# A transformer layer whose first two x tiles are loaded transposed and centred through TensorE, with the other second flips of segment 0 by DMA, merged small operations and a new timetable

## The chip, the cores and the metric

One core of a Trainium2 chip runs the whole program. The metric is the device time of one execution in microseconds (us); lower is better. Five engines take part, each with its own queue that runs in order: TensorE (PE, with its weight loads PEld), VectorE (DVE), ScalarE (ACT), GpSimd (POOL) and SyncE (SP). SP issues nearly all DMA transfers, in its own order, and an engine that waits holds up everything behind it on the same queue.

## The reference

The layer is a pre-norm transformer block on 2048 tokens of width 576 with 32 heads of 18. Attention runs over four segments of 512 tokens. In a segment it mixes a causal softmax attention with a read of a compressive memory M that the earlier segments have filled.

```python
h = x + _A_ref(_layernorm(x, axis=-1), A_wq, A_wk, A_wv, A_wo, A_beta)
h2 = h + _B_ref(_layernorm(h, axis=-1), B_w1, B_b1, B_w2, B_b2)
...
for s in range(N):
    p = _softmax(logits, axis=-1)
    a_dot = jnp.einsum('bhqk,bhkd->bhqd', p, vs)
    pq = phi(qs)
    num = jnp.einsum('bhld,bhde->bhle', pq, M)
    den = jnp.einsum('bhld,bhd->bhl', pq, z)[..., None] + 1e-06
    o = g * (num / den) + (1.0 - g) * a_dot
    pk = phi(ks)
    M = M + jnp.einsum('bhld,bhle->bhde', pk, vs)
    z = z + jnp.einsum('bhld->bhd', pk)
```

`phi(t)` is `where(t > 0, t + 1, exp(t))`. `_B_ref` is a feed-forward net 576 to 4608 to 576 with a tanh GELU between.

## The kernel before

A segment s has four token tiles of 128 rows. The work on it goes through named stages, and every operation is recorded with a tag (stage, segment, and for segment 0 a part) and a name:

- X: load x, layer norm (`stats`, `rstd`, `apply`), and the normalized tile `xn` turned into columns. For segment 0 and half of segment 1 the turn is nine TensorE transposes per tile (`TX`) with copies out of PSUM; for the others the tile goes to DRAM and comes back by a transposing DMA (`flip`).
- P: the projections `Pk`, `Pq`, `Pv` (18 matmuls each for a tile, on two halves of the array's rows), copied out of PSUM by ACT or DVE. Segment 0 turns its first q/k tile by TensorE (`TQ`) and the other three by flips; the others go through DRAM (`qkst`). `ek`, `rk`, `fk` make phi(k) for the memory.
- A: scores (`st0`, `st`), softmax exponentials on ACT (`exp`, 80 in all, each 128x2048), causal masks (`mask`, on POOL or DVE), value matmuls (`val`), then a 32x32-block transpose out of PSUM (`valT`), a reciprocal and the gate (`rec`, `rec2`), and sums (`comb`, `comb2`). For segments 1 to 3 the memory read: `eg`, `rg`, `pq` make phi(q), `mem` is its matmul.
- M: the memory update. B: output projection (`Po`, `Ro`), residual, second layer norm, and the turn of its result `xn2` into `x2T`. The result is written twice side by side, once by `apply` and its repetition by a copy named `tail`, since the two row halves of the array read the blocks in two orders. C: first feed-forward matmul `F1`, evictions `copy` with the bias on ACT or DVE, and `gelu` over batches of many blocks. D: second matmul `F2`, then the output.

The order of the work is neither found at run time nor left to a compiler. `TIMETABLE` gives for every operation a rank and an engine letter (p, a, d, g, s for PE, ACT, DVE, POOL, SP); `Graph.schedule` sorts by rank and emits the operations in that order. So each engine's queue has the ranks' order, and the time is decided by what waits for what. `PORT`, `OVER`, `SLIP` and the costs in `add` are the numbers of a planner that made the table; at build time they choose buffers, not the order.

The begin of the program is what the change touches most. x tile 0 arrives in two pieces (SP and ACT queues), tile 1 in one. The mean of a row is summed by ACT and DVE together (`sum`, lines 739 and 741), `apply` subtracts it (line 763), nine transposes (line 777) turn the tile, ACT copies it into `xreg`, and the projections (line 873) begin. The scale 1/sigma of these two tiles is applied later, when ACT or DVE copies the projections out of PSUM (lines 656, 660). A copy of one element called `gate` (line 725) holds the second batch of loads (x tiles 2 and 3, the q weights `hT`) until the first x has landed. Eight or nine large matmuls on zeros (`warm`, lines 671 and 673) run before.

Of the kernel before, what the change touches and what calls it, by code (L numbers as in the profile page):

```python
# [21 lines left out]
LETTERS = dict(p="pe", a="act", d="dve", g="pool", s="sp")  # L22
# [27 lines left out]
    "A03st0": "p 299 252 318 271 335 377 362",  # L50
    "A03swap": "g 401 402",
    "A03val": "p 340 346 382 385",
    "A03valT": "d 347 390",
    "A1comb": "d460 d498 g576 g613 g648 g666 g751 g720",
    "A1comb2": "g489 g535 g579 g636 d659 g697 g754 d726",
    "A1eg": "a 342 429 351 445 599 538 650 686",
    "A1exp": "a 355 417 433 476 456 484 504 443 547 518 608 591 527 638 623 560 682 675 691 653",
    "A1flip": "s 341 426 349 410 501 502 529 632",
    "A1mask": "g411 g440 g418 d451 g449 g491 g490 d470 g526 g531 g539 g540 d500 g567 d559 g554 d624 g605 g592 d566 g604 g651 d652 g640 d620 d684 "
        "g708 g688 g676 g692 d671 g654",  # L60
    "A1mem": "p 409 492 427 533 630 641 714 696",
    "A1memT": "d 412 496 430 537 631 645 715 698",
    "A1memfin": "g479 g532 g448 g634 d655 g689 g753 g718",
    "A1oT": "d 730 735 746 770 764",
    "A1pq": "d 358 431 365 486 606 627 678 687",
    "A1rec": "d 414 499 447 614 639 646 719 702",
    "A1rec2": "d 459 497 544 612 644 665 745 710",
    "A1rg": "g 357 428 364 485 542 626 555 679",
    "A1st": "p 344 413 432 466 455 483 503 441 546 511 607 590 525 637 622 558 681 667 690 649",
    "A1swap": "g 727 747",  # L70
    "A1val": "p 452 494 541 580 633 662 728 704",
    "A1valT": "d 458 495 543 581 643 663 733 706",
    "A2comb": "d837 d900 d942 g929 d963 g1027 d1061 g1085",
    "A2comb2": "g838 g904 d960 d930 d967 d1029 g1075 g1090",
    "A2eg": "a 768 716 755 828 912 898 945 1014",
    "A2exp": "a 729 737 760 705 771 881 848 834 878 871 903 928 917 972 954 978 956 1010 1018 1040",
    "A2flip": "s 707 617 709 742 823 830 920 882",
    "A2mask": "g738 d752 d756 g761 g763 g721 g788 g772 g893 g868 d894 d854 g889 d879 d888 g872 g943 g952 d939 d918 d982 d980 g965 d979 g985 g973 "
        "g1002 g1035 g1053 g1056 g1079 g1041",
    "A2mem": "p 791 741 905 842 931 1008 1015 1086",  # L80
    "A2memT": "d 792 744 907 843 935 1011 1024 1087",
    "A2memfin": "d795 g821 d958 d906 g966 g1028 g1074 d1089",
    "A2oT": "d 994 995 1030 1096 1104",
    "A2pq": "d 775 717 874 833 913 990 1007 1072",
    "A2rec": "d 793 762 908 844 936 1020 1026 1088",
    "A2rec2": "d 827 861 941 922 962 998 1060 1082",
    "A2rg": "g 748 642 713 783 909 953 959 1063",
    "A2st": "p 725 736 759 703 769 880 845 829 873 850 886 927 914 971 948 977 955 1006 1017 1039",
    "A2swap": "g 1098 1091",
    "A2val": "p 824 825 896 890 957 983 1037 1080",  # L90
    "A2valT": "d 826 840 940 915 961 993 1038 1081",
    "A3comb": "d1155 g1205 g1275 d1245 d1349 g1362 d1441 d1417",
    "A3comb2": "d1183 g1206 d1305 d1254 d1352 g1400 d1450 g1429",
    "A3eg": "a 1036 1109 1214 1167 1185 1319 1267 1383",
    "A3exp": "a 1103 1118 1067 1100 1084 1221 1231 1176 1200 1187 1303 1250 1276 1291 1256 1331 1342 1350 1369 1334",
    "A3flip": "s 981 1057 1102 934 1134 1152 1261 1309",
    "A3mask": "g1133 g1145 g1142 g1114 g1159 g1128 g1158 g1143 g1229 g1248 g1243 g1246 g1210 g1223 d1194 d1236 g1311 d1280 g1268 g1277 g1297 g1323 "
        "g1310 d1308 g1421 d1394 d1395 g1413 d1360 g1406 d1351 g1396",
    "A3mem": "p 1165 1139 1251 1203 1312 1327 1412 1409",
    "A3memT": "d 1168 1140 1257 1204 1313 1328 1414 1420",  # L100
    "A3memfin": "g1182 d1148 g1273 d1237 d1336 d1399 d1419 d1424",
    "A3oT": "d 1306 1307 1401 1452 1455",
    "A3pq": "d 1116 1131 1215 1174 1258 1320 1343 1408",
    "A3rec": "d 1177 1147 1260 1235 1316 1332 1418 1423",
    "A3rec2": "d 1153 1198 1263 1244 1321 1361 1440 1416",
    "A3rg": "g 1108 1105 1141 1169 1195 1262 1339 1366",
    "A3st": "p 1101 1117 1059 1097 1083 1218 1230 1175 1199 1186 1298 1238 1272 1290 1255 1315 1341 1347 1368 1333",
    "A3swap": "a1433 g1453",
    "A3val": "p 1146 1160 1249 1239 1317 1324 1422 1407",
    "A3valT": "d 1149 1197 1259 1240 1318 1355 1432 1415",  # L110
    "B00Po": "p 219",
    "B00Ro": "p 223",
    "B00T": "p 274 284",
    "B00apply": "d 267",
    "B00copy": "d 275 285",
    "B00dma": "s 210",
    "B00hadd": "d 224 227",
    "B00pass": "d 220",
    "B00rstd": "g 266",
    "B00stats": "d 253",  # L120
    "B00tail": "g 273",
    "B01Po": "p 225",
    "B01Ro": "p 232",
    "B01T": "p 276 286",
    "B01apply": "d 256",
    "B01copy": "d 277 287",
    "B01dma": "s 233",
    "B01hadd": "d 237 238",
    "B01pass": "d 226",
    "B01rstd": "g 255",  # L130
    "B01stats": "d 239",
    "B01tail": "d 257",
    "B02Po": "p 463",
# [12 lines left out]
    "B03dma": "s 468",
    "B03flip": "s 589",
    "B03hadd": "d 514 516",
    "B03pass": "g 507",
    "B03rstd": "g 548",  # L150
    "B03stats": "d 521",
    "B03tail": "g 588",
    "B1Po": "p 778 779 856 777",
    "B1Ro": "p 782 789 864 790",
    "B1apply": "d 851 892 933 816",
    "B1dma": "s 757 812 836 794",
    "B1flip": "s 860 921 938 887",
    "B1hadd": "d 784 785 813 814 869 870 796 797",
    "B1pass": "g781 d780 g863 g787",
    "B1rstd": "g 835 891 897 811",  # L160
    "B1stats": "d 786 815 895 798",
    "B1tail": "g859 d911 g937 d853",
    "B2Po": "p 1123 1120 1274 1122",
    "B2Ro": "p 1129 1137 1283 1126",
    "B2apply": "d 1213 1266 1292 1224",
    "B2dma": "s 1154 1062 1253 1031",
    "B2flip": "s 1220 1357 1356 1281",
    "B2hadd": "d 1156 1157 1138 1144 1284 1285 1150 1151",
    "B2pass": "d1127 d1121 g1282 d1125",
# [12 lines left out]
    "B3tail": "g1515 d1561 g1564 g1536",
# [1376 lines left out]
```

## Time and profile before

| what | value |
|---|---|
| median of 3 runs | 449.36 us (448.22 to 450.42) |
| the profiled execution | 449.18 us, of which the profile's span is 447.5 us |
| PE busy | 431.5 us, 96% of the span |
| ACT, DVE, POOL busy | 301.2, 286.9, 180.8 us |
| TensorE clock granted | 1.00 |
| DMA moved | 63.41 MB, mean 142 GB/s |

A profile row reads "start us, duration us, engine, line, operation, out<-in, count [idle before <- what ended it]". Lines of the kernel stand as L873 and so on. PE's rows are pipelined: a row's duration includes the drain, so the distance from one row's start to the next is the better price of a group of matmuls.

### The profile page before, as it was taken

The numbers are of one execution on the slowest core, as the hardware profiler recorded it, in microseconds if no ns is written. First come the engines' busy times: TensorE is split into PE (matmuls) and PEld (weight loads), VectorE is DVE, ScalarE is ACT, GpSimd is POOL, SyncE is SP. The second block draws the span as 40 slices with busy tenths as digits, with TensorE's granted clock in tenths as the row PEclk, the third lists the DMA queues.
The fourth block names the chain that finished last, engine by engine and source line by source line (L and its number), as shares of the span: only waits on it lengthen the run. The fifth ranks groups of instructions, "written<-read, shape, count | busy, mean of one in ns | idle before, by whom it ended". The sixth has DMA issues, their size and how long they took to land. (4 is left out here: it accounts for less than half of the span.)

```text
span 447.5 us, 12499 instructions
## 1 busy us (share of the span) xinstructions
PE 431.5 (96%) x5345; PEld 278.9 (62%) x5346; DVE 286.9 (64%) x623; ACT 301.2 (67%) x261; POOL 180.8 (40%) x319
## 2 busy tenths in 40 slices
PE   6987999899999999999999999999999999999997
PEld 4766677656776676664444766654447775445775
DVE  6899888999889877795678688773774322000012
ACT  6887999898978798775898977563787002566000
POOL 5683867668355833651235265520212111000001
PEclk9999999999999999999999999999999999999999
DMA  7669869999899944861657505404503281340001
GB/s 226 173 134 219 302 216 210 244 260 247 174 285 221 318 159 95 147 130 25 186 162 153 140 4 103 91 4 130 173 1 94 68 198 44 128 149 1 0 15 41
DMA packets 78344, 63.41 MB, mean 142 GB/s; under 512 B 62288, under 2 KB 70096, under 8 KB 78288
## 3 DMA queue, kind: packets, MB, share of 16 engines
q1 hardware_dynamic: 78144, 62.52, 54.9%
q8 instruction: 42, 0.69, 0.7%
q10 hardware_dynamic: 144, 0.09, 0.1%
q14 instruction: 14, 0.11, 0.1%
HBM read 37.36 MB, written 10.29 MB: 106 GB/s over the span
## 5 line engine op out<-in xcount | busy, mean ns | idle before, releaser
L1185 ACT ACTIVATE pt<-bank 128x2048 bf16<-128x2048 f32 x60 | 112.5, 1876 | 32.8 <-PE bank L1181 26.9
L1398 PEld LDWEIGHTS <-hT 128*128 128x128 bf16 x1152 | 110.5, 98 | 34.7 <-issue 6.6
L1312 PE MATMUL bank<-xreg,w1g 64*128 64x512 bf16 x972 | 107.2, 376 | 0.0
L1312 PEld LDWEIGHTS <-w1g 64*128 64x128 bf16 x972 | 46.3, 94 | 57.3 <-issue 2.8
L1398 PE MATMUL bank<-w_lo,hT 128*128 128x288 bf16 x576 | 77.8, 286 | 0.2 <-issue 0.2
L1398 PE MATMUL bank<-w,hT 128*128 128x288 bf16 x576 | 76.8, 286 | 0.6 <-DVE ot L1409 0.6
L1409 DVE TENSOR_TENSOR ot<-bank,hc 128x288 bf16<-128x288 f32 x32 | 14.3, 452 | 90.5 <-PE bank L1398 86.6
L873 PE MATMUL bank<-hT,xreg 64*128 64x288 bf16 x864 | 58.9, 283 | 4.8 <-DMA hT<-in_A_w_dram 2.1
L1196 POOL TENSOR_SCALAR_AFFINE_SELECT pt<-pt 128x512 bf16<-128x512 bf16 x67 | 45.1, 688 | 30.6 <-ACT pt L1185 30.3
L873 PEld LDWEIGHTS <-xreg 64*128 64x128 bf16 x864 | 42.8, 94 | 17.1 <-issue 8.5
L1317 ACT ACTIVATE hT<-bank,b_col 128x512 bf16<-128x512 f32 x36 | 22.6, 687 | 45.6 <-PE bank L1312 45.3
L1327 DVE TENSOR_SCALAR hT<-bank,b_col 128x512 bf16<-128x512 f32 x42 | 30.1, 742 | 21.4 <-PE bank L1312 20.2
L1384 POOL TENSOR_TENSOR hc<-h,b_bc 128x288 f32<-128x288 bf16 x16 | 12.4, 774 | 76.9 <-DVE ot L1409 76.9
L1027 ACT ACTIVATE pt<-bank 128x2048 bf16<-128x2048 f32 x20 | 37.5, 1877 | 6.2 <-PE bank L1024 5.5
L1349 PE MATMUL bank<-xreg,w1g 64*128 64x256 bf16 x648 | 38.6, 269 | 0.5 <-DVE qk_pad L662 0.3
L1349 PEld LDWEIGHTS <-w1g 64*128 64x128 bf16 x648 | 30.8, 94 | 7.0 <-issue 3.6
L1332 ACT ACTIVATE hT<-hT 128x8192 bf16<-128x8192 bf16 (+2 forms) x6 | 31.7, 5318 | 0.2 <-DVE hT L1327 0.2
L1325 ACT ACTIVATE hT<-bank,b_col 128x512 bf16<-128x512 f32 x30 | 19.5, 685 | 16.2 <-PE bank L1312 15.9
L1181 PE MATMUL bank<-qk 32*128 32x384 bf16 (+3 forms) x384 | 23.8, 300 | 1.6 <-DVE v_aug L662 0.9
L753 POOL TENSOR_SCALAR ln<-ln 128x1 f32<-128x1 f32 x32 | 8.8, 277 | 39.2 <-DVE ln L750 39.0
L1226 POOL TENSOR_TENSOR o_nat<-t,t 128x288 bf16<-128x288 f32 x13 | 10.6, 816 | 28.0 <-DVE t L1167 20.4
L1145 DVE SCALAR_TENSOR_TENSOR e<-e,r 128x512 bf16<-128x512 bf16 x24 | 18.9, 788 | 4.0 <-ACT e L1141 3.5
(119 smaller groups left out, 564.2 us busy)
## 6 DMA issues: line engine op xcount, KB each, us to landing
w1g<-in_B_w_dram SPq DMA_DIRECT2D x41, 576.0 KB, 4.4
qkd<-qk_pad SPq DMA_DIRECT2D x12, 512.0 KB, 4.8
w_lo<-in_B_w_dram SPq DMA_DIRECT2D x3, 864.0 KB, 6.6
w<-in_B_w_dram SPq DMA_DIRECT2D x3, 864.0 KB, 6.6
xb<-in_A_x_dram SPq DMA_DIRECT2D x16, 144.0 KB, 3.8
out_dram<-ot SPq DMA_DIRECT2D x15, 144.0 KB, 1.8
x<-in_A_x_dram SPq DMA_DIRECT2D x6, 320.0 KB, 4.5
xnd<-xn SPq DMA_DIRECT2D x10, 160.0 KB, 3.1
```

The costliest lines, as they stand in the source:

```text
L873: nc.tensor.matmul(out=c.t[:, w, 0:HALF], lhsT=xTb.t[r, k, ts], rhs=wt[r, k, :], start=(k == 0), stop=(k == ND - 1))
L1027: ex = add(ps, {"act": 1.88}, lambda e: nc.scalar.activation(out=pt.t[:], in_=st.t[:], func=ACT.Exp, scale=scale), [sc], pt, [st], table=" ...
L1181: nc.tensor.matmul(out=st.t[:, i, off:off + n_], lhsT=qk[rows, 1, kt * P:(kt + 1) * P], rhs=qk[rows, 0, kt * P:L], start=True, stop=True, ...
L1185: ex = add(ps, {"act": 1.88}, lambda e, st=st, pt=pt: nc.scalar.activation(out=pt.t[:], in_=st.t[:], func=ACT.Exp, scale=scale), [sc], pt, ...
L1196: nc.gpsimd.affine_select(out=blk, in_=blk, pattern=[[0, 4], [1, P]], compare_op=ALU.is_ge, fill=0.0, base=0, channel_multiplier=-1)
L1312: nc.tensor.matmul(out=cc[w].t[:], lhsT=w1.t[rows, k, q, :], rhs=x2T[s].t[rows, k, :], start=(k == 0), stop=(k == ND - 1))
L1317: ready_f[f + w] = [add(pf - 12, {"act": 0.68}, lambda e, f=f, w=w, cc=cc: nc.scalar.activation(out=hT[:, :, f + w, :], in_=cc[w].t[:].rea ...
L1325: nc.scalar.activation(out=dst, in_=src, func=ACT.Identity, bias=b)
L1327: nc.vector.tensor_scalar(out=dst, in0=src, scalar1=b, scalar2=None, op0=ALU.add)
L1332: ge = add(2.9, {"act": 0.42 * (f1 - f0) + 0.2}, lambda e, f0=f0, f1=f1: nc.scalar.activation(out=hT[:, :, f0:f1, :], in_=hT[:, :, f0:f1, ...
L1349: nc.tensor.matmul(out=cc[w].t[:, q * 2 * P:(q + 1) * 2 * P], lhsT=w1.t[rows, k, q, :], rhs=x2T[s].t[rows, k, ts], start=(k == 0), stop=(k ...
L1398: nc.tensor.matmul(out=c.t[:, 0:HALF], lhsT=hT[:, tl // 2, f, (tl % 2) * P:(tl % 2 + 1) * P], rhs=w2_c[ch][:, f - ch * WCH, hf * HALF:(hf ...
```

## The change

It has five parts.

1. Segment 0's tiles 0 and 1 come from a second, transposed copy of x, `A_xt`, which the host lays out, straight into `xreg`. TensorE multiplies them by ones (five matmuls for a tile, `cs`), which leaves the column sums on every partition, and DVE subtracts the mean in place (`ctr`, two instructions for a tile). `sum`, `mean`, `apply`, 18 transposes and their copies go. The untransposed rows of both tiles are still loaded (`x01`), for the variance. The warm-up writes ones in place of zeros, one call of it goes, and DVE does the gate's copy.
2. The second norm's result of segment 0, tiles 0 and 1, is turned by flips, as tiles 2 and 3 were; 18 transposes and 4 copies go. `apply` writes both copies of `xn2` in one instruction, on DVE or POOL, and `tail` goes.
3. Small operations are merged or split: the gate factor of `rec2` moves into `comb` (one instruction on DVE, two on POOL); the wide masks of segment 0 become halves.
4. More operations may run on POOL or DVE as the table says: `phi` for `fk` and `pq` on POOL (two instructions there), `apply` of x on POOL, `rk` and `rg` on DVE.
5. The letter t: 24 evictions of C1 and C2 apply the GELU directly on ACT, and the batches leave these blocks out. The whole timetable is new (1704 ranks before, 1688 now), with new planner numbers.

```diff
-    "X00TX": "p 21 22 26 35",
-    "B00T": "p 274 284",
+    "X00cs": "p 11 13",
+    "B00flip": "s 242",
...
-        warm_ok = add(-9.5, {"dve": 0.25}, lambda e: nc.vector.memset(warm[:], 0.0), name="memset")
+        warm_ok = add(-9.5, {"dve": 0.25}, lambda e: nc.vector.memset(warm[:], 1.0), name="memset")
...
-        fill = [warm_up(2, 1.08, [wprev], [Buf(c_s)], 2 * P), warm_up(2, 0.86, [wprev], [Buf(c_s)])]
+        fill = [warm_up(2, 0.86, [wprev], [Buf(c_s)])]
...
+        xt0 = load(-7.9, lambda: xtv(0, 0, KT), lambda: xt_src(0, 0, KT), 164e3, acq=xt)
+        x0b = add(-7.85, {"act": 1.69}, lambda e: nc.scalar.dma_start(out=xtv(0, KT, ND), in_=xt_src(0, KT, ND)), (), None, [xt], name="x0b")
...
+        x1 = add(-7.5, {"sp": 0.45}, lambda e: nc.sync.dma_start(out=xtv(1, 0, ND), in_=xt_src(1, 0, ND)), (), None, [xt], size=295e3, name="x1")
...
+        x01 = add(-7.45, {"sp": 0.45}, lambda e: nc.sync.dma_start(out=x0.t[:], in_=x[0:2 * P, :].rearrange("(j p) d -> p j d", p=P)), (), x0, size=325e3, name="x01")
...
+                    def sums(e, c=c, tl=tl):
+                        for k in range(KT):
+                            r = slice(0, 64 if k == KT - 1 else P)
+                            nc.tensor.matmul(out=c.t[:, 0:P], lhsT=warm[r, 0:P], rhs=xtv(tl, k, k + 1)[r, 0, :], start=(k == 0), stop=(k == KT - 1))
+
+                    def centre(e, k0, k1, c=c, tl=tl):
+                        nc.vector.scalar_tensor_tensor(out=xtv(tl, k0, k1), in0=c.t[:, 0:P].unsqueeze(1).to_broadcast([P, k1 - k0, P]), scalar=-1.0 / D,
+                                                       in1=xtv(tl, k0, k1), op0=ALU.mult, op1=ALU.add)
...
+        def phi(e, out, ek, rk):
+            if e == "dve":
+                nc.vector.scalar_tensor_tensor(out=out, in0=ek, scalar=1.0, in1=rk, op0=ALU.min, op1=ALU.add)
+                return
+            nc.gpsimd.tensor_scalar(out=ek, in0=ek, scalar1=BIG, scalar2=1.0, op0=ALU.min, op1=ALU.min)
+            nc.gpsimd.tensor_tensor(out=out, in0=ek, in1=rk, op=ALU.add)
...
-                    nc.vector.tensor_scalar(out=r1.t[:], in0=r1.t[:], scalar1=omg_q[:, g:g + 1], scalar2=None, op0=ALU.mult)
...
+                        nc.vector.scalar_tensor_tensor(out=t1.t[:, :, 0:Dh], in0=t1.t[:, :, 0:Dh], scalar=omg_q[:, g:g + 1], in1=rb, op0=ALU.mult, op1=ALU.mult)
...
-                ap = layernorm(p0, lambda h=h: h.t[:], [prev], h, xn2, 0.48, later)
-                by_dma = s > 0 or tl in DMA_FLIP_0
...
+                ap = layernorm(p0, lambda h=h: h.t[:], [prev], h, xn2, 0.60, later, twice=True)
...
-                                    nc.scalar.activation(out=dst, in_=src, func=ACT.Identity, bias=b)
+                                    nc.scalar.activation(out=dst, in_=src, func=ACT.Gelu_apprx_tanh if me[0].straight else ACT.Identity, bias=b)
```

DVE, the first rows of the program. `ln` holds the norm's sums, `x_64` is the buffer of tiles 0 and 1 in rows, `xn` the centred tile, `xreg` the transposed tiles, `pt_71` the warm-up's operand. Before:

```order
L636 MEMSET mhalf 128x1
L666 MEMSET pt_71 128x256
L636 MEMSET v_aug_112 128x128
L741 TENSOR_REDUCE ln_102<-x_64 128x1
L744 TENSOR_SCALAR ln_102<-ln_102 128x1
L763 TENSOR_SCALAR xn_139<-x_64,ln_102 128x640
L741 TENSOR_REDUCE ln_103<-x_64 128x1
L744 TENSOR_SCALAR ln_103<-ln_103 128x1
L763 TENSOR_SCALAR xn_140<-x_64,ln_103 128x640
L749 BN_STATS ln_103<-x_64 128x6 x2
```

The same place now:

```order
L638 MEMSET mhalf 128x1
L638 MEMSET v_aug_112 128x128
L730 CAST mark<-xreg 1x1
L668 MEMSET pt_71 128x512
L743 BN_STATS ln_102<-x_64 128x6 x2
L744 BN_AGGR ln_102<-ln_102 128x2
L743 BN_STATS ln_103<-x_64 128x6 x2
L744 BN_AGGR ln_103<-ln_103 128x2
L804 SCALAR_TENSOR_TENSOR xreg<-bank,xreg 128x640 x2
L804 SCALAR_TENSOR_TENSOR xreg<-bank,xreg 128x512 x2
L743 BN_STATS ln_104<-x_65 128x6 x2
```

The statistics of tiles 0 and 1 moved ahead of the work that PE waits for, and the warm-up's memset moved behind the gate's copy, which waits for the first transposed tile.

SP, the first loads. `hT` holds the weights at this time: 1440 and 1152 columns are the k weights, 2592 the q weights. Before:

```order
L640 DMA x_64<-in_A_x_dram 128x288
L705 DMA x_64<-in_A_x_dram 128x640
L640 DMA hT<-in_A_w_dram 128x1440
L640 DMA hT<-in_A_w_dram 128x1152
L640 DMA x_65<-in_A_x_dram 128x640 x2
L640 DMA hT<-in_A_w_dram 128x2592
```

Now:

```order
L642 DMA xreg<-in_A_xt_dram 128x640
L714 DMA x_64<-in_A_x_dram 128x2x640
L712 DMA xreg<-in_A_xt_dram 128x1152
L642 DMA hT<-in_A_w_dram 128x1440
L642 DMA hT<-in_A_w_dram 128x1152
L642 DMA x_65<-in_A_x_dram 128x640 x2
L642 DMA hT<-in_A_w_dram 128x2592
```

Tiles 0 and 1 are loaded twice, once in columns and once in rows, ahead of the weights; the ACT queue carries 128x512 of the columns (128x352 of the rows before).

POOL, from the norm of tiles 2 and 3 (`x_65`) to the first masks (`pt`). `ek` and `rk` are the two inputs of phi(k), `fk_pad` its result. Before:

```order
L753 TENSOR_SCALAR ln_103<-ln_103 128x1
L754 TENSOR_TENSOR ln_103<-ln_103,mhalf 128x1
L933 TENSOR_SCALAR rk_91<-qk_pad_133 128x576
L933 TENSOR_SCALAR rk_91<-qk_pad_134 128x576
L1459 COPY omg_q<-omg_bc 32x8 x4
L753 TENSOR_SCALAR ln_106<-ln_106 128x1
```

Now:

```order
L748 TENSOR_TENSOR ln_105<-ln_105,mhalf 128x1
L760 TENSOR_SCALAR xn_139<-x_65,ln_105 128x640
L1481 COPY omg_q<-omg_bc 32x8 x4
L893 TENSOR_SCALAR ek_90<-ek_90 128x576
L894 TENSOR_TENSOR fk_pad_135<-ek_90,rk_91 128x32x18
L747 TENSOR_SCALAR ln_106<-ln_106 128x1
```

An `apply` and both steps of a `phi` stand on POOL, where the two `rk` stood.

More of the change, by code (lines that the diff above doesn't have):

```diff
@@ L425, in schedule @@
             done.add(op)
+            if op.name == "gelu" and not op.cost["act"]:
+                op.start = op.end = max(self.seen(a, e) for a in op.after)
+                continue
             if op.fence is not None and op.fence.fused:
@@ L479, in seen, with meet @@
     @staticmethod
+    def meet(e, kind, other):
+        dve, pool = (kind, other) if e == "dve" else (other, kind)
+        return bool(dve) or not pool
+    @staticmethod
     def seen(a, e):
@@ L490 @@
     A_x: bass.AP,
+    A_xt: bass.AP,
     A_w: bass.AP,
```

217 lines of the change are left out of this document (111 added, 106 removed), and 575 rows, old and new, of the table TIMETABLE.

## The prediction

> **What bounds the kernel now.** I read the page's first part, then stretches by stage, since a mean over the program hides which stage is limited. Columns: length, busy time of PE, PEld, DVE, ACT, POOL, then the granted clock, the DMA share and GB/s.
>
> ```profile
> span 447.5 us, 12499 instructions
> PE 431.5 (96%) x5345; PEld 278.9 (62%) x5346; DVE 286.9 (64%) x623; ACT 301.2 (67%) x261; POOL 180.8 (40%) x319
> ...
> 0.00:17.00 17.00, 13.38 (x169) 9.22 (x171) 11.32 (x36) 11.89 (x22) 8.92 (x28) 1.00 0.70 211
> 17.00:120.00 103.00, 94.76 (x1747) 68.25 (x1746) 95.29 (x200) 91.95 (x76) 71.04 (x130) 1.00 0.91 223
> 120.00:270.00 150.00, 149.62 (x1812) 92.50 (x1810) 116.49 (x247) 124.06 (x92) 71.90 (x116) 1.00 0.62 156
> 270.00:447.50 177.50, 173.75 (x1627) 108.91 (x1624) 63.78 (x142) 73.28 (x74) 28.89 (x46) 1.00 0.28 76
> ```
>
> PE sets the time: it idles 16.0 us in all. Of these 3.62 lie before 17, 8.24 in 17 to 120, 0.38 in 120 to 270, 3.75 after. So an edit helps only if it takes work from PE or idle from one of the first two stretches; from 120 on, work taken from ACT or DVE alone buys next to nothing. PE's waits in 17 to 120 (who is waited for; total us, times, longest):
>
> ```profile
> PE bank L873 <- DVE qk_pad L662: 1.8, 3, 1.0
> PE bank L1024 <- DVE MZacc L968: 1.7, 1, 1.7
> PE bank L1024 <- ACT pt L1027: 1.3, 4, 0.4
> PE bank L1181 <- DVE v_aug L662: 0.9, 1, 0.9
> PE bank L1181 <- ACT pt L1185: 0.7, 3, 0.3
> PE bank L873 <- DVE v_aug L662: 0.5, 1, 0.5
> PE bank L1349 <- DVE qk_pad L662: 0.3, 1, 0.3
> PE bank L1349 <- DVE hT L1360: 0.2, 1, 0.2
> PE bank L1024 <- ACT pt L1185: 0.2, 1, 0.2
> PE bank L873 <- DVE MZacc L970: 0.2, 1, 0.2
> PE bank L873 <- ACT pt L1027: 0.2, 1, 0.2
> ```
>
> DVE is named for 3.9 us besides the single 1.7, ACT for 2.4. DVE, busy 95.3 of 103, is the first suspect there. The 1.7 is misnamed, as the timeline shows:
>
> ```profile
> 31.02 1.23 SPq L647 DMA_TRANSPOSE w_lo<-qk_pad  x1
> ...
> 32.93 2.94 SPq L647 DMA_TRANSPOSE w_lo<-qk_pad  x1
> ...
> 36.76 0.44 DVE L968 COPY MZacc<-bank 128x304 f32<-128x304 f32 x1
> ...
> 37.24 0.40 PE L1024 MATMUL bank<-w_lo 32*128 32x128 bf16 x16 [1.66 <-DVE MZacc L968]
> ...
> 55.56 1.27 PE L777 MATMUL bank<-ident,xn 128*128 128x128 bf16 x18
> 56.76 0.61 PE L1056 MATMUL bank<-pt,v_aug 128*19 128x256 bf16 x16
> ```
>
> The scores read `w_lo`, which the flip issued at 32.93 writes. From its issue to the scores are 4.3 us; so this wait is SP's queue and the DMA, not DVE.
>
> **The change part by part.** A, the start. The rows that price it:
>
> ```profile
> 1.28 2.74 PE L671 MATMUL bank<-pt 128*128 128x512 bf16 x6 [1.28 <-DVE pt L666]
> ...
> 3.25 0.45 DVE L741 TENSOR_REDUCE ln<-x 128x1 f32<-128x288 bf16 x1 [1.47 <-DMA x<-in_A_x_dram]
> ...
> 3.81 0.42 PE L673 MATMUL bank<-pt 128*128 128x256 bf16 x1
> ...
> 4.52 1.14 PE L777 MATMUL bank<-ident,xn 128*128 128x128 bf16 x9 [0.29 <-DVE xn L763]
> ...
> 5.48 0.81 DVE L749 BATCH_NORM_STATS2 ln<-x 128x6 f32<-128x288 bf16 x2
> ...
> 5.97 0.67 PE L777 MATMUL bank<-ident,xn 128*128 128x128 bf16 x9
> ...
> 6.57 2.38 PE L873 MATMUL bank<-hT,xreg 64*128 64x288 bf16 x36
> ...
> 11.01 2.38 PE L873 MATMUL bank<-hT,xreg 64*128 64x288 bf16 x36 [2.06 <-DMA hT<-in_A_w_dram]
> ...
> 16.03 0.40 PE L1024 MATMUL bank<-qk 32*128 32x128 bf16 x16
> ...
> 16.78 1.87 ACT L1027 ACTIVATE pt<-bank 128x2048 bf16<-128x2048 f32 x1
> ...
> 1.80:11.00 9.20, 6.87 (x63) 4.08 (x62) 6.52 (x20) 6.40 (x14) 4.69 (x13) 1.00 0.86 266
> ...
> L935 DVE SCALAR_TENSOR_TENSOR fk_pad<-ek,rk 128x576 bf16<-128x576 bf16 x12 | 9.5, 794 | 0.0
> ```
>
> The gate's copy now stands ahead of the warm-up's memset and waits for the first x, here 3.25; the memset ends about 3.8. Four large matmuls at the start's pitch of 0.42 ((3.81 - 1.28)/6) end at 5.5, ten `cs` at L777's 0.127 each at 6.8. Meanwhile DVE does the statistics of both tiles (two at 1.0 with the aggregate, from the landing of their rows, which I put at 4.6, 1.3 after the first columns, by their double size) until 6.6, then four `ctr` at L935's price, scaled by width to 0.7 to 0.85: 3.0 us, until 9.8. The first projection can start near 7.5 instead of 6.57. This is still covered: in before PE waits 2.06 us for the q weights at 11.01, and only k projections stand ahead of them. What is not covered are these weights. SP brings 160 + 320 + 288 KB and ACT's queue 128 ahead of them where there were 72 + 88 + 160: 576 KB (590,000 bytes) more, in a stretch that moved 266 GB/s at share 0.86: 2.2 us. I take 13.0 for their landing. From there to the first scores were 5.0 us (11.01 to 16.03), and the order puts nine more transposes into it, 0.6 by 5.97 to 6.57: 18.6. The scores come 2.6 later; the nine transposes have then left the stretch behind, so the loss is **+2.0**. Ends: +0.5 if the extra bytes fit into the idle seventh of the DMA engines (1.3 us of 9.2) and the transposes no longer precede; +3.5 if the POOL `apply` of tile 3, behind four `rstd`, comes after the weights.
>
> B, PE work removed after the start: the 18 transposes of `xn2` ran 55.56 to 56.76, **-1.2**, and one pair of full-row passes less, estimated at -0.1. Their copies' time goes from DVE and ACT into term C. The two flips that replace them cost SP 1.2 us of issue each (the row at 31.02), with loads of weights queued behind, in a stretch where the DMA engines are busy to 0.91. What reads them, the first feed-forward matmuls, stands a segment's value matmuls later, and I cost it at nothing. If that cover is gone, those matmuls wait, at worst 4.3 us each as at 37.24.
>
> C, idle in 17 to 120. Prices for what goes to POOL:
>
> ```profile
> L933 POOL TENSOR_SCALAR rk<-qk_pad 128x576 bf16<-128x576 bf16 x12 | 8.1, 671 | 7.3 <-DVE r L1074 3.3 <-ACT qk_pad L656 2.0 <-DVE qk_pad L662 1.9
> ...
> L1143 POOL TENSOR_SCALAR r<-qk 128x512 bf16<-128x512 bf16 x24 | 15.0, 629 | 3.7 <-DVE e L1145 2.9 <-DMA qk<-qkd 0.5
> ...
> L1384 POOL TENSOR_TENSOR hc<-h,b_bc 128x288 f32<-128x288 bf16 x16 | 12.4, 774 | 76.9 <-DVE ot L1409 76.9
> ...
> L765 DVE TENSOR_SCALAR xn<-x,ln 128x640 bf16<-128x640 bf16 x14 | 9.3, 670 | 0.6 <-POOL ln L754 0.5
> ...
> L765 DVE TENSOR_SCALAR xn<-x,ln x14: 392/442/1231, 9.4 to 99.6; 128x640 bf16<-128x640 bf16 x14
> ```
>
> POOL takes 8 `fk` (0.67 + 0.77 each, 11.5 us), 5 `pq` of segment 1 (0.63 + 0.77, 7.0), 12 `apply` of x (0.69, 8.3) and a few of `xn2`; with `rk`, `rg`, `tail` and some `comb` gone (about 10) its load there rises by 18, from 71 to 89 of 103. DVE falls by 14 to 81: 8 `fk` at 0.79, 5 `pq` alike, 12 `apply` at 0.67 go, and the gate's separate multiply of segment 0; `rk`, `rg` and halves of masks come. DVE's 3.9 of waits go but 0.5 (-3.4). The wait at `w_lo` loses half (-0.8), since SP's last such flip still stands behind loads of weights. POOL's longer steps bring new ones, which I put at +0.5, about one DVE wait of the list. **-3.7**, between -6 (all of 8.24 but the 2.4 named for ACT) and +3 (below).
>
> The last row, minimum, median and maximum of one instruction, shows 392 ns beside 1231: the mean, 670, is 278 above the least. The Trainium skill's page "SBUF — State Buffer" (the part on practical consequences) has VectorE and GpSimd share one port pair that an instruction holds to its end while the other blocks. The spread agrees with that. By the page the 25 or so moved instructions may be held up on POOL in their turn, an estimate of 25 x 0.28 = 7 us; the sum would then be that of the rival with GpSimd as the bound, +3.2, where the rows alone give -3.0.
>
> D, the GELU applied directly: ACT saves 24 blocks' passes and loads two more tables, all past 120, where PE idles 0.38 of 150 us. Nothing; if ACT were late there, those 0.38 would show it. The end (3.75 idle) is untouched.
>
> Sum: +2.0 - 1.3 - 3.7 = -3.0. The profiled execution took 449.18, 1.68 over its span and 0.18 under the median. So the span becomes 444.5 and the time **446.2**.
>
> **The rivals.**
>
> No change. The named waits are a chain's last link; with DVE earlier, PE may wait for ACT, which is busy 91.95 of 103 in the same stretch, and now begins its exponentials 2.6 later. For it: 2.4 us are ACT's already, and ACT's own work ahead of each exponential falls by only 2 to 3 us. Against: 11 us of ACT are free there. DVE's waits then come back under ACT's name. With C at -0.5 the sum is 2.0 - 1.3 - 0.5 = +0.2: 449.4.
>
> Slower: GpSimd becomes the bound in 17 to 120. DVE at 95 of 103 shows where waits begin; POOL at 89, and each of 25 moved instructions 278 ns longer (the excess of L765), would stand at 96. The masks stand between exponential and value matmul, in the same queue as `apply` and `phi`. Then DVE's 3.4 go, POOL brings 3.9 as DVE did and 2.0 more, since a late mask holds PE at once, and the flip's wait stays: C = +2.5, sum +3.2, 452.4. It decides from 95 us of POOL in that stretch. The page named above speaks for it; against it, POOL's own row L1143 has a mean of 629 with DVE as busy as it is.
>
> A start worse than bounded: the q weights at 14.5, since the rows of x for the variance and the columns cross many short packets; +4.0 instead of +2.0 gives 448.2.
>
> **How the numbers follow.** A measurement of this kernel can tell about 0.5%, here 2.2 us: faster is below 447.1, slower above 451.6. The likeliest has 0.52 (own range 443.5 to 448), no change 0.30, GpSimd 0.13, the start 0.05. Faster: 0.46 of the likeliest and 0.02 of the rest, 0.48. Slower: 0.11 of GpSimd's, 0.05 of no change, 0.01 of the likeliest, 0.17 and a little for the start: 0.18. Same: 0.34. The range runs from 442.0 (A at +0.5, C at -6 would be 442.4) to 452.5, the GpSimd case's time; outside it about a seventh is left.
>
> **What would show it.** A: the first exponential over 128x2048 starts near 19 (16.78 would mean A is nothing), PE's wait for `hT` at the start ends near 13. B: no transposes of `xn` near 55, and no PE wait for `xreg` at the first feed-forward matmuls. C: PE idle between the first exponential and 120 falls from 8.2 to about 4.5, POOL is busy near 89 there and DVE near 81, the DVE names vanish from the waits; if POOL's stand in their place the third case holds, if ACT's, the second. The forecast is wrong if the q weights land by 11 (then it is some 2 us faster), or if POOL passes 95.

## The result

The changed kernel takes 491.31 us (median of 4 runs, 489.96 to 492.53), the kernel before 449.75: a ratio of 1.093, 95% interval 1.089 to 1.097. The forecast was 446.2, with a range of 442.0 to 452.5 and a chance of 0.18 for slower. The page of the changed kernel, then two of its stretches (length, busy time of PE, PEld, DVE, ACT, POOL, clock, DMA share, GB/s):

```profile
span 490.8 us, 12469 instructions
...
PE 442.3 (90%) x5324; PEld 282.6 (58%) x5325; DVE 284.4 (58%) x563; ACT 297.5 (61%) x276; POOL 296.0 (60%) x367
...
17.00:120.00 103.00, 77.64 (x1370) 54.19 (x1370) 66.21 (x147) 69.63 (x64) 97.38 (x126) 0.89 0.72 181
120.00:270.00 150.00, 139.92 (x1828) 88.65 (x1824) 116.02 (x213) 117.57 (x97) 114.92 (x132) 0.98 0.63 161
```

POOL is busy 296.0 us, 180.8 before. In 17 to 120 it is busy 97.4 of 103, and every other engine has become idler: PE 94.8 to 77.6, DVE 95.3 to 66.2, ACT 92.0 to 69.6. That is how a new bound looks. Behind 120, in 150 us, POOL goes from 71.9 to 114.9. The span grew by 43.3: PE's idle from 16.0 to 48.5 (32.5), its busy time by 10.8, though it has less to do. PE's waits in the whole program say for whom. The three largest, apart from the warm-up's 4.6 at the start (who is waited for; total us, times, longest):

```profile
PE bank L1072 <- POOL pt L1056: 7.6, 4, 4.4
PE bank L1167 <- POOL MZ_blk L992: 6.2, 1, 6.2
...
PE bank L1371 <- DMA xreg<-xn: 4.1, 1, 4.1
```

In all POOL is named for 20.1 us (six entries); in the kernel before no wait of 0.2 or more names it. POOL's groups, shapes kept apart (behind the bar: busy us, mean ns of one):

```profile
L760 POOL TENSOR_SCALAR xn<-h,ln 128x1152 bf16<-128x1152 bf16 x9 | 39.6, 4404 | 2.2 <-DMA xreg<-xn 1.6
L760 POOL TENSOR_SCALAR xn<-x,ln 128x640 bf16<-128x640 bf16 x12 | 31.3, 2609 | 0.9
L893 POOL TENSOR_SCALAR e<-e 128x512 bf16<-128x512 bf16 x12 | 23.2, 1932 | 7.9 <-ACT e L1157 7.0
L893 POOL TENSOR_SCALAR ek<-ek 128x576 bf16<-128x576 bf16 x8 | 18.2, 2275 | 0.8 <-ACT ek L947 0.3
L894 POOL TENSOR_TENSOR e<-e,r 128x512 bf16<-128x512 bf16 x12 | 14.2, 1181 | 1.0
L894 POOL TENSOR_TENSOR fk_pad<-ek,rk 128x576 bf16<-128x576 bf16 x8 | 10.4, 1302 | 0.7
L949 POOL TENSOR_SCALAR rk<-qk_pad 128x576 bf16<-128x576 bf16 x6 | 4.0, 665 | 0.1
```

One of these lines by single instructions (minimum/median/maximum, in ns):

```profile
L760 POOL TENSOR_SCALAR xn<-x,ln x12: 2513/2522/3125, 12.9 to 115.6; 128x640 bf16<-128x640 bf16 x12
```

One `apply` of x takes 2.61 us where I had 0.69, the limit of phi 1.93 and 2.28 where I had 0.63 and 0.67, its sum 1.18 and 1.30 where I had 0.77; one `rk` takes 0.67, as before. The moved work is 137 us in these six groups; by my prices it would be some 47 (1.2 taken for an `apply` of `xn2`, which I had left without one). The least and the median of `apply` are 9 ns apart: most of them do not wait for another engine, they are simply this long. What one such instruction does to PE is seen at one wait, in the timeline of POOL:

```profile
85.57 2.52 POOL L760 TENSOR_SCALAR xn<-x,ln 128x640 bf16<-128x640 bf16 x1
88.03 1.23 POOL L1056 TENSOR_SCALAR_AFFINE_SELECT pt<-pt 128x512 bf16<-128x512 bf16 x2
...
89.89 0.64 POOL L1056 TENSOR_SCALAR_AFFINE_SELECT pt<-pt 128x512 bf16<-128x512 bf16 x1
```

And of PE, with the granted clock in two stretches of 1 us (the last figure but two):

```profile
90.58 0.60 PE L1072 MATMUL bank<-pt,v_aug 128*19 128x128 bf16 x10 [4.41 <-POOL pt L1056]
91.12 3.38 PE L1371 MATMUL bank<-xreg,w1g 64*128 64x256 bf16 x36
...
94.76 2.14 PE L1371 MATMUL bank<-xreg,w1g 64*128 64x256 bf16 x36
...
91.00:92.00 1.00, 1.00 (x16) 0.65 (x12) 0.70 (x1) 0.00 (x0) 0.92 (x3) 0.50 1.05 274
94.00:95.00 1.00, 1.00 (x24) 0.53 (x20) 0.47 (x1) 0.06 (x1) 1.00 (x1) 1.00 0.91 169
```

The masks stand in POOL's queue behind an `apply`, the value matmuls behind the masks. And a wait costs twice: the 36 matmuls after it take 3.38 us, the next 36 of the same kind 2.14. The granted clock is 0.50 behind the wait and 1.00 again from 94 on; over 17 to 120 it is 0.89. The Trainium skill's page "TensorE: Matmul & The Clock Gate" (Part 1) has the clock fall to half after an idle window of about 3.4 us. This wait of 4.41 agrees with that; a shorter one, shown under "The start" below, does not.

### The profile page after: what moved, and what is told of

Same layout as the page of the kernel before. It is cut to its first block, busy times and chain, and to the rows that moved or that the text cites. A ratio compares the mean times of both kernels' runs of the same rounds, so it can differ in the third digit from the quotient of the medians.

```text
span 490.8 us, 12469 instructions
## 1 busy us (share of the span) xinstructions
PE 442.3 (90%) x5324; PEld 282.6 (58%) x5325; DVE 284.4 (58%) x563; ACT 297.5 (61%) x276; POOL 296.0 (60%) x367
## 4 chain that ended last, share of the span: by engine, by line
PE 46%; DVE 4%; issue 1%; POOL 1%; ACT 1%; ACTq 0%; DVEq 0%
PE bank L1421 22%; PE bank L1333 20%; PE bank L841 2%; PE bank L1196 1%; PE bank L1222 1%; DVE pt L1209 1%; DVE t L1182 1%; ACT pt L1200 1%; DVE ot L1432 0%; DVE t L1230 0%; PE bank L867 0%; DVE t L1176 0%; POOL e L893 0%; PE bank L1167 0%; DVE t L1239 0%
## 5 line engine op out<-in xcount | busy, mean ns | idle before, releaser
L1333 PEld LDWEIGHTS <-w1g 64*128 64x128 bf16 x972 | 47.2, 94 | 57.0 <-issue 3.1
L882 PE MATMUL bank<-hT,xreg 64*128 64x288 bf16 x864 | 61.8, 294 | 3.0 <-DVE qk_pad L664 3.0
L1338 ACT ACTIVATE hT<-bank,b_col 128x512 bf16<-128x512 f32 x36 | 22.6, 689 | 47.3 <-PE bank L1333 47.1
L1371 PE MATMUL bank<-xreg,w1g 64*128 64x256 bf16 x648 | 41.9, 284 | 4.6 <-DMA xreg<-xn 4.1
L760 POOL TENSOR_SCALAR xn<-h,ln 128x1152 bf16<-128x1152 bf16 x9 | 39.6, 4404 | 2.2 <-DMA xreg<-xn 1.6
L1371 PEld LDWEIGHTS <-w1g 64*128 64x128 bf16 x648 | 32.8, 99 | 12.7 <-issue 7.4
L1296 ACT ACTIVATE hT<-hT 128x1024 bf16<-128x1024 bf16 (+7 forms) x19 | 38.4, 2092 | 0.1
L1348 DVE TENSOR_SCALAR hT<-bank,b_col 128x512 bf16<-128x512 f32 x31 | 22.3, 733 | 27.8 <-PE bank L1333 27.8
L1346 ACT ACTIVATE hT<-bank,b_col 128x512 bf16<-128x512 f32 x41 | 25.9, 687 | 19.9 <-PE bank L1333 19.6
L760 POOL TENSOR_SCALAR xn<-x,ln 128x640 bf16<-128x640 bf16 x12 | 31.3, 2609 | 0.9
L893 POOL TENSOR_SCALAR e<-e 128x512 bf16<-128x512 bf16 x12 | 23.2, 1932 | 7.9 <-ACT e L1157 7.0
L1196 PE MATMUL bank<-qk 32*128 32x128 bf16 (+3 forms) x384 | 24.9, 308 | 1.0 <-ACT pt L1200 0.5
```

Source lines behind the costliest of these rows:

```text
L760: VEC[e].tensor_scalar(out=dst, in0=frm, scalar1=sm.t[:, 12:13], scalar2=sm.t[:, 15:16], op0=ALU.subtract, op1=ALU.mult)
L882: nc.tensor.matmul(out=c.t[:, w, 0:HALF], lhsT=xtv(tl, k, k + 1)[r, 0, :] if xTb is xt else xTb.t[r, k, ts], rhs=wt[r, k, :], start=(k == ...
L893: nc.gpsimd.tensor_scalar(out=ek, in0=ek, scalar1=BIG, scalar2=1.0, op0=ALU.min, op1=ALU.min)
L1196: nc.tensor.matmul(out=st.t[:, i, off:off + n_], lhsT=qk[rows, 1, kt * P:(kt + 1) * P], rhs=qk[rows, 0, kt * P:L], start=True, stop=True, ...
L1296: nc.scalar.activation(out=view(r0, r1), in_=view(r0, r1), func=ACT.Gelu_apprx_tanh)
L1333: nc.tensor.matmul(out=cc[w].t[:], lhsT=w1.t[rows, k, q, :], rhs=x2T[s].t[rows, k, :], start=(k == 0), stop=(k == ND - 1))
```

## The experiments

The theories: P, the moved instructions are long by the pair of operations they do, and GpSimd is the bound; L, they are held up by VectorE at a shared port; O, the order itself, with its start and its flips, costs the time.

**Forms alone.** The kernel before with instructions of this kind appended behind its last work:

```diff
+        for _ in range(2):
+            g.tensor_scalar(out=A, in0=B, scalar1=BIG, scalar2=0.0, op0=ALU.min, op1=ALU.max)
+            g.tensor_scalar(out=C, in0=C, scalar1=BIG, scalar2=1.0, op0=ALU.min, op1=ALU.min)
...
```

> The kernel before, with 28 GpSimd instructions of 128x512 bf16 appended behind its last work, when VectorE is nearly idle (they write scratch that nothing reads). Theory P (price): an instruction of GpSimd costs what its pair of operations costs, whoever else runs: limit from above then below (min 3e38, max 0) 0.61 us as now, (min, min) and (subtract, mult) 1.9 us, tensor_tensor add 1.15. Theory L (lock): the long ones in the changed kernel were held up by VectorE; alone all of them take 0.6 to 0.7. Open: which other pairs are short (min 1 then max 0; one operation alone; mult then add). The time of the whole is about 449 plus some 35 of appended work under P, plus 18 under L.

Its one execution took 485.9 us, 36 more than the kernel before (449.6), as P has it. The lines: 1499 (min, max 0); 1500 and 1501 (min, min) in place and not; 1502 (min 1, max 0); 1503 (max 0, min 1); 1504 min alone; 1505 add alone; 1506 mult by a column alone; 1507 and 1508 (subtract, mult) by columns and by constants; 1509 and 1510 (mult, add) by columns and by constants; 1511 the sum of two tensors. Nine of them:

```profile
L1499 POOL TENSOR_SCALAR pt<-pt 128x512 bf16<-128x512 bf16 x2 | 1.2, 614 | 0.1
L1500 POOL TENSOR_SCALAR pt<-pt 128x512 bf16<-128x512 bf16 x2 | 3.9, 1933 | 0.2
L1502 POOL TENSOR_SCALAR pt<-pt 128x512 bf16<-128x512 bf16 x2 | 1.2, 614 | 0.2
L1503 POOL TENSOR_SCALAR pt<-pt 128x512 bf16<-128x512 bf16 x2 | 3.8, 1920 | 0.2
L1505 POOL TENSOR_SCALAR pt<-pt 128x512 bf16<-128x512 bf16 x2 | 3.0, 1506 | 0.2
L1507 POOL TENSOR_SCALAR pt<-pt,ln 128x512 bf16<-128x512 bf16 x2 | 4.2, 2085 | 0.2
L1509 POOL TENSOR_SCALAR pt<-pt,ln 128x512 bf16<-128x512 bf16 x2 | 1.5, 770 | 0.2
L1510 POOL TENSOR_SCALAR pt<-pt 128x512 bf16<-128x512 bf16 x2 | 1.2, 620 | 0.2
L1511 POOL TENSOR_TENSOR pt<-pt,pt 128x512 bf16<-128x512 bf16 x2 | 2.3, 1150 | 0.2
```

VectorE is idle here but for one instruction, and the long forms are as long as in the changed kernel. L falls. Two pairs are short: min then max, and mult then add, at 0.61 to 0.77 us for 512 columns. Each other pair measured takes 1.92 to 2.09, one operation alone 1.50 to 1.57; the same two operations in the other order, max then min, 1.92. `rk` uses min with a bound of 3e38 and then max, which is the short pair. In both short rows of min then max the second bound is 0, so whether another bound there is as short is not shown.

**Which of the moves costs.** The changed kernel with `apply`, with phi, and with both given back to VectorE at their ranks:

```diff
+        if op.eng == "pool" and name == "apply":       # or in ("fk", "pq"), or all three
+            op.eng = "dve"
```

> The changed kernel with its 21 apply instructions of GpSimd given to VectorE at the same ranks. P: GpSimd loses 12 x 2.6 + 9 x 4.4 = 71 of its 296 us and the time falls to 460 to 470. Theory O (the order itself, the start and the flips cost the time): it stays above 480. L: about 480, since what is left on GpSimd keeps its price and VectorE gets more to fight over.

> The changed kernel with its 20 phi steps (fk, pq) of GpSimd given to VectorE at the same ranks, as one instruction each. P: GpSimd loses 12 x 3.1 + 8 x 3.6 = 66 us; the time falls to 462 to 472. O: above 480.

> Both moves undone. P: GpSimd is busy near 160, its waits vanish, the time is 447 to 455; what is over 449.8 is then the start (the first large exponential stands at 21.5 in the changed kernel, 16.8 before). O: above 470.

Measured: 468.04 (ratio 1.043, 1.039 to 1.047), 488.64 (1.088, 1.084 to 1.093) and 467.20 (1.042, 1.038 to 1.046). The apply is worth 23 us, as P says; phi only 3 where P said 20 or more, and 1 with apply already back; both back leave 17 us where P said 0 to 5. Neither O nor P as I had put it holds. With both back GpSimd is busy 162 us and no wait of PE of 0.2 or more names it, so it isn't the bound, and still PE waits. VectorE's timeline of both_on_dve, and PE's waits:

```profile
77.10 1.05 DVE L762 TENSOR_SCALAR xn<-x,ln 128x640 bf16<-128x640 bf16 x1 [3.66 <-POOL ln L750]
78.07 0.54 DVE L1055 TENSOR_TENSOR pt<-pt,tri 128x512 bf16<-128x512 bf16 x1
```

```profile
PE bank L1074 <- DVE pt L1055: 6.5, 2, 4.1
```

VectorE stands 3.66 us before an `apply` whose 1/sigma GpSimd hasn't made, with a mask behind it that PE needs; 2.4 of the 6.5 us are the wait for this mask. These ranks place the work where GpSimd would do it; on the other engine's queue the same rank blocks other things. That this makes up all of the 17 us is not shown. So undoing an engine's letter alone does not undo the change, and a cleaner test keeps ranks and engines and takes the length alone.

**Short pairs, same order.**

```diff
-            nc.gpsimd.tensor_scalar(out=ek, in0=ek, scalar1=BIG, scalar2=1.0, op0=ALU.min, op1=ALU.min)
+            nc.gpsimd.tensor_scalar(out=ek, in0=ek, scalar1=1.0, scalar2=0.0, op0=ALU.min, op1=ALU.max)
...
+                if e == "pool":
+                    nc.gpsimd.tensor_scalar(out=sm.t[:, 16:17], in0=sm.t[:, 12:13], scalar1=sm.t[:, 15:16], scalar2=-1.0, op0=ALU.mult, op1=ALU.mult)
+                    nc.gpsimd.tensor_scalar(out=dst, in0=frm, scalar1=sm.t[:, 15:16], scalar2=sm.t[:, 16:17], op0=ALU.mult, op1=ALU.add)
+                    return
```

> The changed kernel with its orders untouched; only the pairs of operations on GpSimd differ: phi's limit as (min 1, max 0), the same value since its input is an exponential, and apply as (mult, add) with -mean/sigma made by one more 128x1 instruction. From the forms measured alone (0.61 in place of 1.92, 0.77 in place of 2.08 at 512 columns) GpSimd should lose 17 us in the x applies, 24 in the others and 28 in phi: from 296 to about 227. Theory P (price of the pair): 448 to 455. Theory O (what else the new order does: start, flips, long chains through GpSimd): 460 or more.

> The changed kernel with only apply on GpSimd in the form (mult, add); phi keeps (min, min). GpSimd loses 41 of the 69 us that cheap_forms took from it. If time follows GpSimd's load evenly, 491 - 37 x 41/69 = 469. If the apply, which stands ahead of masks and of transposes and projections that PE waits for, weighs more: 458 to 465; phi's part is then 4 to 11 us.

Measured: 454.26 (1.013, 1.009 to 1.016) and, with the apply's part only, 471.55 (1.050, 1.046 to 1.053). So 37 of the 42 us lie in two pairs of operations, 20 of them in `apply` (39 us of GpSimd) and 17 in phi (27 us): about in the share of the load they take (that would be 22 and 15). So `apply` weighs no more than its load, and the second size that I expected for it (458 to 465) missed. Page and middle stretch of cheap_forms:

```profile
PE 433.1 (96%) x5324; PEld 277.7 (61%) x5325; DVE 266.6 (59%) x563; ACT 296.7 (66%) x276; POOL 230.6 (51%) x388
...
17.00:120.00 103.00, 92.70 (x1706) 64.23 (x1704) 85.12 (x184) 90.38 (x81) 90.11 (x165) 0.98 0.89 219
```

And its waits on PE in that stretch:

```profile
PE bank L1076 <- POOL pt L1060: 3.8, 4, 1.8
PE bank L1171 <- POOL MZ_blk L996: 2.4, 1, 2.4
...
PE bank L1375 <- DMA xreg<-xn: 0.3, 1, 0.3
```

POOL 90 and DVE 85 of 103 are about the loads that I had forecast (89 and 81). PE's idle is 19.7 against 48.5, its busy time 433.1 against 442.3 for the same matmuls: so of the 38.0 us of span between them 28.8 are waits and 9.2 a slower TensorE, whose granted clock over the program is 0.97 in the changed kernel and 1.00 in cheap_forms.

**The reverse, in the kernel before.** Twelve `apply` of x to GpSimd, in the long and in the short pair:

```diff
-    "X2apply": "d 241 183 325 315",
+    "X2apply": "g 241 183 325 315",
...
```

> The kernel before with the same 12 apply instructions of x on GpSimd as in the changed kernel (one of segment 0, three of segment 1, all of segments 2 and 3), in the form (subtract, mult), and nothing else. P: each takes 2.5 us; GpSimd goes from 181 to 211, from 71 to about 100 of 103 between 17 and 120, and the time rises by 8 to 20. O: within 3 of the kernel before, since VectorE gains 8 us.

> The same with (mult, add) and the extra 128x1 instruction: 1.15 us each instead of 2.5. P: most of the loss goes; within 3 of the kernel before, on either side. O: as before_x_on_pool.

Measured: 465.38 (1.036, 1.031 to 1.041) and 454.49 (1.012, 1.007 to 1.016). Twelve instructions of 2.53 us cost 17 us of time; in the short form (1.02, and 0.35 for the extra one) 6, more than the 3 that I allowed, with DVE's load 10 us lower in 17 to 120 (84.7). The stretch and the first wait of the short form:

```profile
17.00:120.00 103.00, 92.42 (x1695) 64.23 (x1691) 84.74 (x186) 87.57 (x76) 84.69 (x152) 0.98 0.89 214
```

```profile
PE bank L1060 <- POOL pt L1044: 5.3, 3, 2.7
```

GpSimd is at 84.7 of 103 there, and PE waits 5.3 for its masks. So masks come late well before GpSimd is full.

**The start.** cheap_forms with the warm-up's memset ahead of the gate:

```diff
-    "memset": "d9 d0 g19 g5 d6 a50 a100 a79 a15 g144 g239 g346",
+    "memset": "d3.5 d0 g19 g5 d6 a50 a100 a79 a15 g144 g239 g346",
```

> The kernel of cheap_forms with the warm-up's memset put ahead of the gate's copy on VectorE, as before the change, so that TensorE begins near 1.3 instead of 4.6. If the late warm-up costs: the first k projection starts near 7.2 instead of 8.6 and the time falls by 0.5 to 1.5 against cheap_forms. If the q weights or the apply of tile 3 set the first scores: no difference (under 0.5).

Measured: 454.01 (1.012, 1.009 to 1.015), 0.25 less, which four executions of each can't tell from nothing. The first large exponential of the changed kernel, of cheap_forms (with its scores), and of this one:

```profile
21.48 1.88 ACT L1042 ACTIVATE pt<-bank 128x2048 bf16<-128x2048 f32 x1
```

```profile
18.96 0.40 PE L1043 MATMUL bank<-qk 32*128 32x128 bf16 x16
...
19.65 1.88 ACT L1046 ACTIVATE pt<-bank 128x2048 bf16<-128x2048 f32 x1
```

```profile
17.98 1.88 ACT L1046 ACTIVATE pt<-bank 128x2048 bf16<-128x2048 f32 x1
```

It comes 1.67 us earlier. Where the lead went is seen at the same wait for a mask in both, first in cheap_forms, then here:

```profile
73.16 0.39 PE L1076 MATMUL bank<-pt,v_aug 128*19 128x128 bf16 x10 [1.84 <-POOL pt L1060]
73.48 2.14 PE L1375 MATMUL bank<-xreg,w1g 64*128 64x256 bf16 x36
```

```profile
71.81 0.39 PE L1076 MATMUL bank<-pt,v_aug 128*19 128x128 bf16 x10 [1.83 <-POOL pt L1060]
72.14 3.80 PE L1375 MATMUL bank<-xreg,w1g 64*128 64x256 bf16 x36
```

The wait is as long, but here the granted clock behind it is 0.60 (72 to 74) and 0.50 (74 to 75.5), there 1.00, and the 1.66 us of the 36 matmuls eat the lead. Later this execution gets it back: behind cheap_forms' next long wait, 2.37 for `MZ_blk`, its clock is 0.50 (92 to 94), and the two profiled spans end 1.7 apart (452.8 and 451.1). So one execution of each does not show what the start is worth, and the medians leave it open.

**The last 5 us.** From cheap_forms_early_warm, parts of GpSimd's work given to VectorE (by the two lines above, with the names fk, pq, both, and apply in stage B), and then one part left out:

> cheap_forms_early_warm (454.0) with the eight fk given to VectorE. GpSimd loses 16 us, nearly all between 17 and 120 where it is busy 90 of 103; VectorE gains 6.5 on 85. If what is left of the loss (6 us) is GpSimd's load there, in which the add of phi costs 1.27 us where I had 0.77: 450 to 452.5. If the ranks were laid out for GpSimd and VectorE's queue now blocks: 455 or more.

> cheap_forms_early_warm with the twelve pq given to VectorE: GpSimd loses 22 us, five ninths of it behind 120. Load theory: 452 to 454, less than fk brings, since only five lie between 17 and 120. Rank theory: 455 or more.

> Both of them on VectorE: GpSimd near 192 in all and near 72 of 103 between 17 and 120, VectorE near 95 there, as before the change. Load theory: 449 to 452. Rank theory: 456 or more.

> cheap_forms_early_warm with the nine apply of xn2 given to VectorE: GpSimd loses 9 x 1.8 = 16 us, most of it behind 100, VectorE gains 6. Load theory: 452 to 454. Rank theory, by what fk (455.8) and pq (464.1) did on VectorE: 456 or more.

```diff
-            nc.gpsimd.tensor_scalar(out=ek, in0=ek, scalar1=1.0, scalar2=0.0, op0=ALU.min, op1=ALU.max)
             nc.gpsimd.tensor_tensor(out=out, in0=ek, in1=rk, op=ALU.add)
```

> cheap_forms_early_warm (454.0) with phi's first step on GpSimd, the limit at 1, left out (so phi is exp + max(x, 0) there); ranks and engines stay. It takes 13.8 us from GpSimd, about 9 of them between 17 and 120, and puts nothing on VectorE. If what is left of the loss is GpSimd's load: 448 to 451.5. If it lies elsewhere (start, colder TensorE, stages behind 120): 453 or more.

Measured: 455.81 (fk; 1.015, 1.011 to 1.018), 464.05 (pq; 1.033, 1.029 to 1.037), 463.09 (both; 1.032, 1.027 to 1.036), 456.19 (apply of xn2; 1.017, 1.014 to 1.019); the load theory missed all four and the rank theory's bounds held, though GpSimd fell to as little as 195 us. With pq on VectorE, that engine stands 3.1 us at one pq for GpSimd's `r`, and PE 3.4 for a transpose behind it. Left out in its place, the limit of phi, 14 us of GpSimd, brings 448.19 (0.999, 0.997 to 1.001), equal to the kernel before:

```profile
96.16 0.69 DVE L897 SCALAR_TENSOR_TENSOR e<-e,r 128x512 bf16<-128x512 bf16 x1 [3.11 <-POOL r L1165]
```

```profile
PE bank L888 <- DVE t L1182: 3.4, 1, 3.4
```

```profile
17.00:120.00 103.00, 95.31 (x1788) 67.29 (x1782) 88.90 (x190) 94.12 (x82) 87.93 (x160) 1.00 0.98 231
```

The first two rows are of cheap_pq_on_dve, the last of cheap_no_limit: PE 95.3 busy, as before the change (94.8). So the last 5 to 6 us, too, go if work leaves GpSimd, and not if it is moved to VectorE at the same rank. The instruction left out also stood in the chain that leads to the memory's matmuls; whether its place in the chain or GpSimd's load counts more, this run doesn't separate.

**The wait at `w_lo`.** In the kernel before, one load moved behind the flip:

```diff
-    "dma": "s 2 9 14 60 51 192 101 283",
+    "dma": "s 2 9 14 60 51 196.5 101 283",
```

> The kernel before with one rank changed: SP issues the load of the output weights wt_o behind the last flip into w_lo instead of ahead of it. If PE's 1.66 at 37.24 was the flip's landing: the flip is issued 0.6 earlier, that wait falls to about 1.0 and the time by 0 to 0.6. If it was VectorE's copy that the profile names: nothing. Both are near what can be measured; the wait in the trace decides.

Measured: 449.42 (1.001, 0.999 to 1.003). The rows:

```profile
37.24 0.09 PEld L1024 LDWEIGHTS <-w_lo 32*128 32x128 bf16 x1 [0.43 <-DMA w_lo<-qk_pad]
...
38.13 0.44 DVE L968 COPY MZacc<-bank 128x304 f32<-128x304 f32 x1
...
38.62 0.40 PE L1024 MATMUL bank<-w_lo 32*128 32x128 bf16 x16 [1.50 <-DVE MZacc L968]
```

The same weight load in the kernel before:

```profile
35.52 0.09 PEld L1024 LDWEIGHTS <-w_lo 32*128 32x128 bf16 x1 [0.24 <-issue]
```

Measured from the scores, the last flip is issued 0.6 us earlier than before, and the wait stays, 1.50. In both kernels PE had already begun to load weights from `w_lo` when it waited, 1.4 us ahead of the matmuls here, 1.7 in the kernel before. The flip issued at 32.93 in the kernel before landed 6.1 us later, at 39.0, behind these scores: they can't have waited for it. In both kernels the scores begin 0.04 to 0.05 us after VectorE's copy ends (36.76 + 0.44, 38.13 + 0.44). The name in the profile was right.

No version here beats the kernel before by what can be measured; cheap_no_limit, which leaves the limit of phi out, equals it.

## Why the prediction was wrong, step by step

- **C, the prices on GpSimd: this step failed.** I priced `apply` (subtract, mult) and the limit (min, min) by `rk` (min, max), the row with engine, shape and instruction name alike. What counts is the pair, and the row doesn't show it; the code does. The sum of two tensors I took from L1384 at 0.77, which is a row of 288 columns, for 512 and 576: 1.18 and 1.30 were measured. Together the six groups took 137 us where these prices give 47, and with the short pairs, all else kept, 37 of the 42 us went. The Trainium skill's page "GPSIMD Engine Reference" (Elementwise) gives about 2.6 cycles per element for two inputs at 1.2 GHz; by it 576 columns are an estimate of 1.25 us, and the trace agrees with that.
- **C, bounds.** The upper end, +3, was set from DVE's waits, not from a bound on the prices themselves. No row of before showed these pairs on GpSimd, so the range had to ask what happens if they cost several times as much. Twelve `apply` at 2.53 us took 17 us by themselves in the reverse test.
- **The rival with GpSimd as the bound** named the mechanism, the place (masks in the queue behind `apply` and `phi`) and the sign (95 of 103; it stood at 97). Its price, 278 ns more for each, was taken from VectorE's waits, and its result, 452.4, was 39 short. Nor is 95 where it begins: at 90 in cheap_forms PE waits 6.2 us for POOL in that stretch.
- **The shared port** was the wrong reason: GpSimd's long forms are as long with VectorE idle. The longest `apply` of x, 3.12 us where most take 2.52, did run beside an `fk` of VectorE (28.27 and 28.32), but 0.6 us is all that shows. VectorE waits in turn, as one of its lines in the changed kernel shows:

```profile
L891 DVE SCALAR_TENSOR_TENSOR fk_pad<-ek,rk x4: 746/896/3137, 28.3 to 149.9; 128x576 bf16<-128x576 bf16 x4
```

  The Trainium skill's page "SBUF — State Buffer" (Who interferes with whom) has the second to issue block until the first ends. The instruction of 3.14 us, 0.90 at the median, agrees nearly: it ran from 149.92 to 153.06 beside an `apply` of GpSimd from 148.52 to 152.80. The pair at 28.27 doesn't fit as well: there the one whose row starts first was the longer.
- **A, the start.** The first scores were to come 2.6 us later, at 18.6, because of the q weights. In the changed kernel the first large exponential came 4.7 later (21.48 against 16.78), and not because of them: PE ran 54 projections, k and then q, from 8.60 to 12.08 without a wait, so the q weights had landed by about 11, the sign that I had named for a wrong forecast. With `apply` on VectorE PE waited 0.65 for them, until 11.66, not 13.0:

```profile
11.66 1.28 PE L884 MATMUL bank<-hT,xreg 64*128 64x288 bf16 x18 [0.65 <-DMA hT<-in_A_w_dram]
```

  What was late was the first projection (8.60, where I had 7.5) and then the chain statistics, `ctr`, statistics, 1/sigma, `apply`, TensorE turns. In the changed kernel GpSimd's `apply` of tile 3, which I had named for the worse end, stands in it with 2.68 us:

```profile
15.61 1.14 PE L773 MATMUL bank<-ident,xn 128*128 128x128 bf16 x9 [2.54 <-POOL xn L760]
```

  With the short pairs the scores come at 18.96, with `apply` on VectorE at 18.00. That lies near my 18.6, but for another reason, so it is luck. No run shows how much of this delay reaches the end.
- **B.** The transposes went. The cover that I had named was gone in the changed kernel, with a wait of 4.1 us for `xreg` (I had 4.3 as the worst for one), since the flip, issued at 70.46, came behind an `apply` of 4.27 us on GpSimd that ended at 70.44; with the short pairs 0.3 are left.
- **C, the flip's wait** was misread: a wait is not misnamed because a DMA was also under way, and the flip that I named landed after the scores. That the scores start within 0.05 us of the named copy's end, in the row I quoted, was the sign.
- **D, after 120,** was counted as nothing; PE idles 10.1 of 150 there instead of 0.38, with POOL at 114.9. Of these 2.5 us name POOL. Two waits of 1.5 and 1.6 name DVE, which itself stood behind POOL: 1.84 us for an `ln`, and in the 3.14 above. The rest is open. ACT, whose GELU D was about, is named for 0.5. A PE without idle shows only that the present load of the others is hidden.

## What to carry to other kernels

Before work is moved to another engine, look for a row of that engine doing the same operations, not just the same instruction on the same shape; where there is none, leave the range open upward, or measure a dozen forms behind the kernel's end in one run. A rank or a place in a queue belongs to the engine it was laid out for: to test a price, change the length of the work with order and engines kept. And a saving counts only where PE waits for what it speeds up: in the reverse test VectorE had 10 us less to do in its fullest stretch, and the time rose, since PE waited for GpSimd.

## What the runs showed of the hardware

- GpSimd's tensor_scalar over 128x512 bf16 takes 0.61 us for (min, max), 0.62 for (mult, add) with constants and 0.77 with columns, but 1.92 to 2.09 for every other pair tried, (max, min) among them, and 1.50 to 1.57 for one operation. By the two widths of `apply` (2.52 at 640, 4.28 at 1152, medians) a long pair costs 3.4 ns a column. So two operations can be shorter than one. Min then max was measured with 0 as the second bound only.
- TensorE after an idle of 4.41 us is slower for the next 3.4 us: the same 36 matmuls took 3.38 and 2.14 us, at a granted clock of 0.50 at first and 1.00 later. A wait of 1.83 us could do the same (3.80, cheap_forms_early_warm) or one of 1.84 leave it at 1.00 (2.14, cheap_forms): the length of a single wait does not decide it. Between the changed kernel and cheap_forms TensorE's busy time for the same matmuls differs by 9.2 of 38.0 us.
